# Five z2 normalizes on ScalarE, and three mixing passes of the second token tile written ahead of the last pass of the first

## The chip, the cores and the metric

One core of a Trainium2 chip runs one launch of the kernel. The metric is the device time of that launch in microseconds (us); lower is better. A core has TensorE (PE: matmuls, with PEld for its weight loads), VectorE (DVE), ScalarE (ACT), GpSimd (POOL) and SyncE (SP), which here issues nearly all DMAs. Each engine works through its own queue in order, and an instruction that waits holds up all behind it on its engine.

## The reference

The kernel computes x + A(xn) + B(xn), with xn the layer norm of x (2048 tokens, 512 columns, bf16).

```python
def A(x, wqkv, wo):            # sliding dilated attention: 32 heads of 16, window 8, dilation 2
    q, k, v = heads(x @ wqkv)
    logits = einsum('bhsd,bhswd->bhsw', q, kg) * scale     # kg, vg: k, v at s, s-2, ..., s-14
    attn = softmax(where(mask, logits, -1e9))
    return einsum('bhsw,bhswd->bhsd', attn, vg).reshape(B, S, D) @ wo

def B(x, w_in, w_sp, b_sp, w_out):                         # gated MLP with mixing over tokens
    z = gelu(x @ w_in)                                     # 2048 x 1376
    z1, z2 = z[..., :688], layernorm(z[..., 688:])
    g = einsum('ts,bsf->btf', w_sp, z2) + b_sp[None, :, None]
    return (z1 * g) @ w_out
```

## The kernel before

All tensors stay in SBUF; 2048 tokens are 16 tiles of 128. A tile is named by (j, tb), where tb is one of four blocks of 512 tokens and j one of the four tiles in it. The work of all engines is written out by hand, in one string, `ORDER` (line 41): each word is a step, and the steps are issued in the order of the words. A step puts its instructions at the end of the queues of its engines; there is no scheduler that would change the order. A table `steps` (line 717) maps the first letters of a word to a function.

The steps that matter here, with their engine and line:

- `V`, `X`, `z`, `q` (TensorE): matmuls for v (L431), z1 and z2 (L263), q and k (L321).
- `Vc` and `Xg` (ScalarE): they empty the PSUM tile of a `V` (L437) or, through gelu, of an `X` (L312).
- `zg`, `zs` (ScalarE): gelu of z2 with its sum (L281), square with its sum (L287). `st.0` to `st.4` make mean and 1/std of all 16 tiles from these (L290 to L300).
- `Nj.tb` (VectorE, L304): the normalize of tile (j, tb) of z2, in place: subtract the mean, multiply by 1/std. There are 16.
- `Gn` (TensorE, L470): the mixing matmuls for output tile n, 32 of them in four passes of eight. Pass b, written `Gn.b`, reads the z2 tiles with j = b; in `Gn` alone all four follow each other. `Gin` (ScalarE, L476) adds the bias and empties the PSUM tile; `Un` (VectorE, L484 and L486) multiplies by z1; `Tn` (SyncE, L490) transposes the product by DMA.
- `pg.c`, `ag`, `bg` (VectorE, L361, L370, L373): products of q and k and their sums for group g of the attention. `Lg` (TensorE, L381) sums them over the head's 16 columns into logits, and `Lcg` (ScalarE, L387) empties these.
- `M0.k` (VectorE, L395 to L401), `E0` (ScalarE, L405), `S0.0` to `S0.2` (VectorE, L410 to L414), `S0.3` and `S0.4` (ScalarE, L417 and L420), `R0` (VectorE, L424): the softmax of the first half of the token tiles: maximum, exp, sum, reciprocal as exp of -ln, scaling. `M1`, `E1`, `S1`, `R1` are the second half.
- `An` (VectorE, L445 and L449): attention weights times v, 60 steps.
- `O`, `Or`, `Oh`, `Of` (TensorE, L523, L532, L553): the two output projections, added up in one PSUM tile for each block of 128 tokens. `Or` reads the transposed products that the `T` steps land. `Fe`, `F`, `s` (ScalarE L536, VectorE L541 and L543, SyncE L548) empty it, add x and store.
- `wn` (SyncE, L461): loads the rows of w_sp for `Gn`, transposed. Loads reuse each other's space, so that `w6` waits for the end of `G0`.

Two more things set the order. The gelu and exp functions on ScalarE need different tables, and a table load stands in ScalarE's queue where the kind changes (ahead of `Xg6`, of `E0`, and so on). The PSUM tiles of `V`, `X`, `q`, `z` and `G` come from one pool of three buffers, those of `L` from a pool of two: a matmul that takes a buffer waits until the step on ScalarE that empties it has ended. The matmuls of `L7` take the buffer that `Lc5` gives back.

Of the kernel before, what the change touches and what calls it, by code (L numbers as in the profile page):

```python
# [8 lines left out]
F32 = mybir.dt.float32  # L9
ACT = mybir.ActivationFunctionType  # L10
ALU = mybir.AluOpType
# [3 lines left out]
P = 128  # L15
S = 2048
D = 512
NT = S // P
# [26 lines left out]
b2 zg0.2 zs3.3 L0 L1 Xg4 q3.1 p3.2 zs3.1 p3.0 Lc0 q3.0 Lc1 p3.1 qc3.1 q3.2 p3.3 qc3.0 zs0.1 a3 z0.3 qc3.2 q3.3  # L45
zg0.3 p4.1 zs1.3 p4.0 z0.0 qc3.3 X1 p4.2 zg0.0 zs0.3 X2 p4.3 Xg1 X5 st.0 zs2.1 st.1 a4 Xg2 L2 V6 zs0.2 zs3.2
b3 Xg5 V2 b4 Vc6 zs0.0 p5.3 L3 V5 zs3.0 p5.2 Vc2 V1 st.2 p5.1 Vc5 p5.0 V0 st.3 a5 w4 Lc2 Vc1 V4 st.4 Vc0 w1
N1.1 V3 N2.0 Vc4 N1.0 b5 Lc3 V7 N0.0 Vc3 M0.0 N1.2 M0.1 L5 N0.2 L4 Vc7 N3.3 X6 N0.1 M0.2 N0.3 late X3 N3.1
N1.3 N2.1 G0.0 N2.2 Xg6 N2.3 N3.2 N3.0 G0.1 p7.1 G0.2 M0.3 G0.3 p7.2 G4 p6.0 Gi0 w6 Lc4 p6.3 Xg3 p6.2 E0 p7.3
G3 p6.1 U0 S0.0 p7.0 a6 w9 G1 Gi3 Gi4 S0.1 b6 a7 G2 Gi1 w7 U1 S0.2 b7 S0.3 w5 S0.4 Lc5 R0 L6 L7 G6 Lc6 A0 Gi2  # L50
Lc7 U2 U4 mask T4 U3 M1.0 A1 T2 G7 A2 Gi6 w8 A3 wo1.2 A4 T0 A5 X7 M1.1 Gi7 A6 wo1.3 xr0 G5 A7 Xg7 A8 w10 M1.2
A9 w12 U7 A10 X8 Gi5 A11 X10 T1 A12 G8 Xg10 A13 Xg8 wo1.0 A14 T7 M1.3 A15 G9 Gi8 A16 A17 E1 A18 A19 wo0.2
# [17 lines left out]
def kernel(  # L70
# [13 lines left out]
    V = nc.vector  # L84
    A = nc.scalar
# [8 lines left out]
    sb = ctx.enter_context(tc.tile_pool(name="sb", bufs=1))  # L94
# [44 lines left out]
    z2 = sb.tile([P, NT, FH], BF16, name="z2")  # L139
# [15 lines left out]
    zmean = sb.tile([P, NT], F32, name="zmean")  # L155
    zm2 = sb.tile([P, NT], F32, name="zm2")
    zvar = sb.tile([P, NT], F32, name="zvar")
    zrstd = sb.tile([P, NT], F32, name="zrstd")
    eps_t = sb.tile([P, 1], F32, name="eps_t")
    mhalf = sb.tile([P, 1], F32, name="mhalf")  # L160

# [127 lines left out]
    def z2_var():  # L289
        return [lambda: V.tensor_scalar(zmean[:], zsum[:], 1.0 / FH, None, ALU.mult),  # L290
                lambda: V.tensor_tensor(zm2[:], zmean[:], zmean[:], ALU.mult),
                lambda: V.scalar_tensor_tensor(zvar[:], zsq[:], 1.0 / FH, zm2[:], ALU.mult, ALU.subtract)]
# [9 lines left out]
    def z2_norm(j, tb):  # L302
        i, q = 4 * tb + j, 4 * j + tb
        V.tensor_scalar(z2[:, i, :], z2[:, i, :], zmean[:, q:q + 1], zrstd[:, q:q + 1], ALU.subtract, ALU.mult)  # L304

    def z1_mm(n):
        tiles["x", n] = zmm(4 * (n % 4) + ORD[n // 4], w_z1)
# [99 lines left out]
    def sm_sum(hf, k):  # L407
        a = a_sb[:, :, 256 * hf:256 * hf + 256]
        if k == 0:
            V.tensor_tensor(smt[:], a[:, 0:4, :], a[:, 4:8, :], ALU.add)  # L410
        elif k == 1:
            V.tensor_tensor(smt[:, 0:2, :], smt[:, 0:2, :], smt[:, 2:4, :], ALU.add)
        elif k == 2:
            V.tensor_tensor(smt[:, 0, :], smt[:, 0, :], smt[:, 1, :], ALU.add)  # L414
        elif k == 3:
            need_table("exp")
            A.activation(smt[:, 1, :], smt[:, 0, :], ACT.Ln)  # L417
        else:
            need_table("exp")
            A.activation(srec[:], smt[:, 1, :], ACT.Exp, scale=-1.0)  # L420
# [290 lines left out]
    def halo_zero():  # L711
# [3 lines left out]
    st = z2_var() + [z2_log, z2_exp]  # L715

    steps = {"z": z2_mm, "zg": z2_gelu, "zs": z2_sq, "q": qk_mm, "qc": qk_cast, "p": prod_c, "a": pair_add, "b": pair_add2,
             "L": logits, "Lc": logits_cast, "V": v_mm, "Vc": v_cast, "X": z1_mm, "Xg": z1_gelu,
             "st": lambda k: st[k](), "N": z2_norm,
             "M": sm_max, "E": sm_exp, "S": lambda h, k: sm_sum(h, k), "R": sm_norm, "mask": add_mask,  # L720
             "G": g_mm, "Gi": g_bias, "U": u_mul, "T": u_tr, "A": lambda k: ap[k](),
             "O": out_heads, "Or": out_rest, "Oh": out_half, "Of": out_first, "Fe": out_evac, "F": out_add, "s": out_store, "end": last_adds,
             "halo": halo_zero, "wo": load_wo, "late": load_late, "xr": load_xr, "w": load_wsp}
    for tok in ORDER.split():
        name = tok.rstrip("0123456789.")
# [31 lines left out]
```

## Time and profile before

| what | value |
|---|---|
| time, median of 3 runs | 201.84 us (201.63 to 201.85) |
| span of the profiled execution | 199.9 us, 4102 instructions |
| time around the span (median less span) | 1.94 us |
| TensorE busy | 195.4 us, 98% |
| VectorE busy | 184.6 us, 92% |
| ScalarE busy | 103.9 us, 52% |
| GpSimd busy | 22.0 us, 11% |
| 16 normalizes (L304) | 6.4 us, 0.460 us each |
| 16 bias steps (L476) | 13.2 us, 0.834 us each |
| mixing matmuls, first and last start (L470) | 77.7 and 180.0 us |

The span runs from the first to the last instruction of one profiled execution; starts are counted from its begin. A timeline line gives start, length, engine, source line, operation, output and inputs, and in brackets the idle time of the engine before it and what ended that. Several equal instructions in a row are one line with their count, and its length is that of the whole row; instructions of an engine overlap a little, so that the distance from start to start is less than the length of one.

### The profile page before, as it was taken

How to read it: one execution, taken by the hardware profiler on the slowest of the kernel's cores; microseconds unless marked ns; L12 is line 12 of the kernel's file. 1: busy time of each engine (PE TensorE's matmuls, PEld its weight loads, DVE VectorE, ACT ScalarE, POOL GpSimd, SP SyncE). 2: the span in 40 equal slices, each digit the busy share in tenths (PEclk: the TensorE clock that was granted, in tenths of full speed). 3: DMA queues.
4: the chain of work that ended last, by engine and by line, in shares of the span. 5: the costliest groups of instructions: out<-in, count | busy, mean ns of one | idle time of the engine just before them, and what ended most of it. 6: DMA issues, size and time to landing. Idle time of an engine off the chain costs nothing.

```text
span 199.9 us, 4102 instructions
## 1 busy us (share of the span) xinstructions
PE 195.4 (98%) x1691; PEld 123.9 (62%) x1691; DVE 184.6 (92%) x249; ACT 103.9 (52%) x175; POOL 22.0 (11%) x23
## 2 busy tenths in 40 slices
PE   7899999999999999999999999999999999999994
PEld 2869756665566666666656666666544646664562
DVE  5789899999999999999979999999999999999624
ACT  3586978899899976453431523708402230331400
POOL 3000800699500000000000000000000000000000
DMA  5986548950000096524477999199940297219863
GB/s 160 266 244 163 106 78 240 234 113 3 0 0 3 3 157 115 167 64 100 61 152 161 239 220 192 49 217 180 192 85 0 81 208 169 72 32 127 215 209 105
DMA packets 66562, 25.91 MB, mean 130 GB/s; under 512 B 56496, under 2 KB 66288, under 8 KB 66288
## 3 DMA queue, kind: packets, MB, share of 16 engines
q1 hardware_dynamic: 65824, 25.18, 58.4%
q10 hardware_dynamic: 720, 0.48, 0.8%
q8 instruction: 13, 0.21, 0.4%
q14 instruction: 5, 0.04, 0.1%
HBM read 10.13 MB, written 2.10 MB: 61 GB/s over the span
## 4 chain that ended last, share of the span: by engine, by line
PE 95%; DMA 1%; DVE 1%; SPq 0%; ACT 0%; issue 0%
PE pg L470 37%; PE pz L263 19%; PE pq L321 11%; PE pv L431 7%; PE po L553 7%; PE po L523 6%; PE pa L553 2%; PE pq L327 2%; DMA r_x<-in_A_x_dram 1%; PE pl L381 1%; PE pa L321 1%; PE po L532 1%; PE pb L523 1%; PE pt L238 0%; DVE r_pr L541 0%; DVE stats L213 0%
## 5 line engine op out<-in xcount | busy, mean ns | idle before, releaser
L470 PE MATMUL pg<-z,r_qk 128*128 128x344 bf16 x448 | 66.8, 309 | 0.0
L470 PEld LDWEIGHTS <-r_qk 128*128 128x128 bf16 x448 | 43.8, 98 | 22.0 <-issue 0.4
L445 DVE TENSOR_TENSOR r_pr<-r_x,r_w 128x2048 bf16<-128x2048 bf16 x32 | 38.4, 1220 | 1.3 <-PE pl L381 1.0
L263 PE MATMUL pz<-w_z,xnT 128*128 128x344 bf16 x256 | 39.3, 309 | 0.0
L449 DVE TENSOR_TENSOR r_pr<-r_pr 128x2048 bf16<-128x2048 bf16 x28 | 33.9, 1219 | 0.4
L263 PEld LDWEIGHTS <-xnT 128*128 128x128 bf16 x256 | 25.0, 98 | 13.2 <-issue 0.4
L476 ACT ACTIVATE gs<-pg,b_col 128x688 bf16<-128x688 f32 x16 | 13.2, 834 | 35.4 <-PE pg L470 26.4
L361 DVE TENSOR_TENSOR r_pr<-r_qk 128x2048 bf16<-128x2048 bf16 x24 | 27.9, 1222 | 0.2 <-ACT r_qk L337 0.2
L321 PE MATMUL pq<-xnT,r_w 128*128 128x512 bf16 (+1 forms) x128 | 23.8, 339 | 0.0
L321 PEld LDWEIGHTS <-r_w 128*128 128x128 bf16 x144 | 15.9, 114 | 7.6 <-issue 0.4
L536 ACT CAST r_qk<-po 128x512 bf16<-128x512 f32 x10 | 5.5, 588 | 22.7 <-PE po L553 22.7
L699 POOL CAST b_col<-b 128x16 f32<-128x16 bf16 x1 | 15.7, 15704 | 11.8 <-DMA b<-in_B_b_sp_dram 11.8
L337 ACT CAST r_qk<-pq 128x1024 bf16<-128x1024 f32 x15 | 14.9, 1015 | 2.4 <-PE pq L321 2.3
L312 ACT ACTIVATE r_uz<-pz 128x688 bf16<-128x688 f32 x16 | 11.7, 740 | 6.6 <-PE pz L263 6.5
L523 PE MATMUL po<-r_lg,r_pr 32*128 32x512 bf16 x192 | 14.5, 375 | 0.0
L431 PE MATMUL pv<-xnT,r_w 128*32 128x512 bf16 x256 | 14.2, 379 | 0.0
L553 PEld LDWEIGHTS <-r_uz 128*128 128x128 bf16 x85 | 8.0, 98 | 9.5 <-issue 1.1
L370 DVE TENSOR_TENSOR r_pr<-r_pr 128x4096 bf16<-128x4096 bf16 x6 | 13.7, 2289 | 0.0
L553 PE MATMUL po<-r_w,r_uz 128*128 128x512 bf16 x60 | 13.6, 380 | 0.0
L281 ACT ACTIVATE z<-pz 128x688 bf16<-128x688 f32 x16 | 11.9, 744 | 1.5 <-PE pz L263 1.5
L287 ACT ACTIVATE junk<-z 128x688 bf16<-128x688 bf16 x16 | 12.4, 774 | 0.1
L431 PEld LDWEIGHTS <-r_w 128*32 128x32 bf16 x256 | 9.5, 138 | 4.3
(88 smaller groups left out, 200.3 us busy)
## 6 DMA issues: line engine op xcount, KB each, us to landing
r_lg<-in_A_wo_dram SPq DMA_DIRECT2D x8, 256.0 KB, 4.2
r_x<-in_A_x_dram SPq DMA_DIRECT2D x12, 128.0 KB, 3.0
out_dram<-r_qk SPq DMA_DIRECT2D x12, 128.0 KB, 2.1
r_w<-in_A_wqkv_dram SPq DMA_DIRECT2D x8, 128.0 KB, 3.6
r_qk<-in_A_x_dram SPq DMA_DIRECT2D x8, 128.0 KB, 2.2
w_z<-in_B_w_in_dram SPq DMA_DIRECT2D x4, 172.0 KB, 4.4
w_z<-in_B_w_in_dram SPq DMA_DIRECT2D x1, 688.0 KB, 5.5
r_w<-in_B_w_out_dram SPq DMA_DIRECT2D x1, 640.0 KB, 6.5
```

Source lines behind the costliest of these rows:

```text
L263: PE.matmul(pz[:, hh, 0:FHALF], xnT[:, kc, i * P:(i + 1) * P], wz[:, kc, hh * FHALF:(hh + 1) * FHALF], start=(kc == 0), stop=(kc == C - 1))
L321: PE.matmul(pq[:, cc, p0 * P:(p0 + b1 - b0) * P], wqk[:, sd, kc, c0 + cc:D:C], xv[:, kc, b0:b1, j, :], start=(kc == 0), stop=(kc == C - 1))
L337: cast = A.copy(dst, pq[:, :, p0 * P:(p0 + b1 - b0) * P].rearrange("p c (b t) -> p c b t", b=b1 - b0))
L361: prod = V.tensor_tensor(pr[g % 3][:, c].rearrange("p w b t -> p b w t"), q3.unsqueeze(2).broadcast_to([P, TB, 4, P]), k4, ALU.mult)
L370: V.tensor_tensor(pr[g % 3][:, 0:2], pr[g % 3][:, 0:2], pr[g % 3][:, 2:4], ALU.add)
L431: PE.matmul(pv[32 * tb:32 * tb + 32, dd, :], wv[:, kc, 2 * d2 + dd, :], xnT[:, kc, tb * TBS:(tb + 1) * TBS], start=(kc == 0), stop=(kc == ...
L445: V.tensor_tensor(pw_t[n], vp[:, :, off:off + P], a_sb[:, slot_w(w), ts].unsqueeze(1).broadcast_to([P, DH, P]), ALU.mult)
L449: V.tensor_tensor(pw_t[n] if dst is None else dst, pw_t[n], pw_t[m], ALU.add)
L470: PE.matmul(pg[:, hh, 0:FHALF], wsp[n][:, k, :], z2[:, k, hh * FHALF:(hh + 1) * FHALF], start=(k == 0), stop=(k == NT - 1))
L523: PE.matmul(pc, op[32 * tb:32 * tb + 32, d, o * P:(o + 1) * P], wo_r[32 * tb:32 * tb + 32, d, cs], start=(d == 8), stop=False, tile_positi ...
L553: mm = PE.matmul(pc, uT[:, o % 2, m, tb * P:(tb + 1) * P], wout[:, m, cs], start=False, stop=(m == MCH - 3))
L699: G.tensor_copy(b_col[:], b16[:])
```

## The change

It has three parts, all in the stretch where the first mixing tiles begin.

1. Five of the sixteen normalizes, (2,3), (3,3), (3,1), (3,2) and (3,0), are no longer done by VectorE but by ScalarE, as an Identity activation with a scale and a bias for each partition. The first two stand ahead of `Xg6` in ScalarE's queue, the other three behind it and ahead of `Gi0`. The order of the normalizes left on VectorE changes a little: (2,2) comes before (1,3) and (2,1).
2. A new step `Z` on VectorE makes the bias, -mean/std of all 16 tiles, in one small instruction between the normalizes.
3. Passes 0, 1 and 2 of `G4` are written ahead of pass 3 of `G0`, and pass 3 of `G4` behind it. Before, all four passes of `G4` followed `G0`. Pass 3 reads the tiles (3, 0) to (3, 3), all four of which are now ScalarE's.

```diff
 ORDER (the rows that change)
-N1.1 V3 N2.0 Vc4 N1.0 b5 Lc3 V7 N0.0 Vc3 M0.0 N1.2 M0.1 L5 N0.2 L4 Vc7 N3.3 X6 N0.1 M0.2 N0.3 late X3 N3.1
-N1.3 N2.1 G0.0 N2.2 Xg6 N2.3 N3.2 N3.0 G0.1 p7.1 G0.2 M0.3 G0.3 p7.2 G4 p6.0 Gi0 w6 Lc4 p6.3 Xg3 p6.2 E0 p7.3
+N1.1 V3 N2.0 Vc4 Z N1.0 b5 Lc3 V7 N0.0 Vc3 M0.0 N1.2 M0.1 L5 N0.2 L4 Vc7 NA2.3 NA3.3 X6 N0.1 M0.2 N0.3 late X3 N2.2
+N1.3 N2.1 G0.0 Xg6 NA3.1 NA3.2 NA3.0 G0.1 p7.1 G0.2 M0.3 G4.0 G4.1 G4.2 G0.3 G4.3 p7.2 p6.0 Gi0 w6 Lc4 p6.3 Xg3 p6.2 E0 p7.3
 G3 p6.1 U0 S0.0 p7.0 a6 w9 G1 Gi3 Gi4 S0.1 b6 a7 G2 Gi1 w7 U1 S0.2 b7 S0.3 w5 S0.4 Lc5 R0 L6 L7 G6 Lc6 A0 Gi2
...
+    zshift = sb.tile([P, NT], F32, name="zshift")
...
+    def z2_shift():
+        V.scalar_tensor_tensor(zshift[:], zmean[:], -1.0, zrstd[:], ALU.mult, ALU.mult)
+
+    def z2_norm_act(j, tb):
+        i, q = 4 * tb + j, 4 * j + tb
+        A.activation(z2[:, i, :], z2[:, i, :], ACT.Identity, bias=zshift[:, q:q + 1], scale=zrstd[:, q:q + 1])
...
-             "st": lambda k: st[k](), "N": z2_norm,
+             "st": lambda k: st[k](), "N": z2_norm, "NA": z2_norm_act, "Z": z2_shift,
```

The row that begins with `G3` is unchanged and is shown because the prediction follows it.

## The prediction

> **What bounds the kernel now.** I read the busy times first, then the chain that ended last, then the busy times by stretch, and at last the timelines of ScalarE, VectorE and SyncE around the change.
>
> ```profile
> PE 195.4 (98%) x1691; PEld 123.9 (62%) x1691; DVE 184.6 (92%) x249; ACT 103.9 (52%) x175; POOL 22.0 (11%) x23
> PE 95%; DMA 1%; DVE 1%; SPq 0%; ACT 0%; issue 0%
> ```
>
> TensorE carries the end: 95% of the chain is matmul. The question is whether it ever waits. In order of time, and by stretch (us, PE busy, PEld, DVE, ACT, POOL, clock, DMA share, GB/s):
>
> ```profile
> 77.82 23.33 PE pg L470 x160
> 101.15 0.55 PE pl L381 x8
> 77.60:101.10 23.50, 23.50 (x166) 15.59 (x167) 22.85 (x26) 9.33 (x12) 0.00 (x0) 1.00 0.51 108
> 101.10:142.60 41.50, 41.50 (x293) 27.45 (x296) 40.66 (x49) 18.38 (x22) 0.00 (x0) 1.00 0.91 173
> ```
>
> From 77.6 to 142.6 it is busy throughout, at full clock. The 160 mixing matmuls take 23.33 / 160 = 0.1458 us each without a gap. So nothing around the change holds TensorE today, and an edit there can only leave the time or add a stall. It has to be found which wait now ends last. The starts below are the timeline's (first G0 matmul 77.65). ScalarE:
>
> ```profile
> 82.58 0.83 ACT L476 ACTIVATE gs<-pg,b_col 128x688 bf16<-128x688 f32 x1 [4.51 <-PE pg L470]
> 83.31 0.59 ACT L387 ACTIVATE r_lg<-pl 128x512 bf16<-128x512 f32 x1
> 83.79 0.75 ACT L312 ACTIVATE r_uz<-pz 128x688 bf16<-128x688 f32 x1
> 84.55 1.28 ACT L272 ACT_TABLE_LOAD   x1
> 85.85 1.91 ACT L405 ACTIVATE r_w<-r_lg 128x2048 bf16<-128x2048 bf16 x1
> 98.34 0.42 ACT L417 ACTIVATE smt<-smt 128x256 f32<-128x256 f32 x1 [0.99 <-DVE smt L414]
> 99.11 0.58 ACT L387 ACTIVATE r_lg<-pl 128x512 bf16<-128x512 f32 x1
> ```
>
> These are Gi0, Lc4, Xg3, the table load, E0 (the first exp), S0.3 and Lc5. The bracket says that Gi0 waited for the end of G0, and the four behind it follow without a gap. VectorE:
>
> ```profile
> 88.75 1.22 DVE L410 TENSOR_TENSOR smt<-r_w 128x1024 f32<-128x1024 bf16 x1
> 94.96 2.29 DVE L370 TENSOR_TENSOR r_pr<-r_pr 128x4096 bf16<-128x4096 bf16 x1
> 97.39 0.49 DVE L484 TENSOR_TENSOR r_uz<-gs,r_uz 128x640 bf16<-128x640 bf16 x1
> 97.89 0.42 DVE L414 TENSOR_TENSOR smt<-smt 128x256 f32<-128x256 f32 x1
> 101.53 1.23 DVE L445 TENSOR_TENSOR r_pr<-r_x,r_w 128x2048 bf16<-128x2048 bf16 x1 [0.95 <-PE pl L381]
> 102.89 0.49 DVE L484 TENSOR_TENSOR r_uz<-gs,r_uz 128x640 bf16<-128x640 bf16 x1
> ```
>
> These are S0.0, a7, U1, S0.2, A0 and U2. S0.0 reads what E0 wrote (E0 ends 87.76).
>
> **Part 1: five normalizes leave VectorE.** Eight in a row took 3.04 us with 0.46 for the last, so one costs (3.04 - 0.46) / 7 = 0.37. Five less is 1.85; the new zshift row (like L292, 0.17, taken as 0.2 with its hand-over) leaves 1.65 us. VectorE reaches U0 that much earlier, and there it waits for Gi0. TensorE gains nothing: the last normalize ended at 79.26 and its pass began at 81.15, 1.9 us later. Worth 0; it cannot be a gain while TensorE is gapless.
>
> **Part 2: five normalizes on ScalarE.** No row shows this form. The nearest are L476 (0.83 long; two take 1.56, so 0.73 apart) and the L287 square of the same SBUF tile (0.77). Bounds 0.60 to 0.95 apart; I take 0.73, since L476 is the same function with a pointer operand. NA2.3 and NA3.3 stand before the gelu table load and push Xg6 by 1.5, to an end near 79.5; G4 takes Xg6's PSUM buffer and is due at 81.15. The other three end near 81.8; G0.3 is due at 84.65. Even 0.95 leaves over a microsecond, so the cost is 0; beyond 1.5 apart the excess of two of them would stop TensorE at G4. No table load is added: L476 runs behind either load today. The Trainium skill ("ScalarE: Activation LUTs", What ACT_TABLE_LOAD costs) gives 186 ns + 0.833 ns per element and 93 ns per pointer operand, an estimate of 0.95 us for 688 elements and two pointers, where the L476 row with one pointer took 0.83; both fit into the idle time.
>
> **Part 3: three passes of G4 ahead of the last of G0.** Three passes are 24 matmuls, 24 x 0.1458 = 3.50 us. G0 ends 3.50 later; TensorE's total is the same. But everything queued behind Gi0 on ScalarE moves by 3.50.
>
> First wait: G3 takes G0's PSUM buffer, because Gi0 gives it back before Xg3 gives back X3's. Gi0 ended 82.58 + 0.83 - 82.17 = 1.24 after G0's last matmul began; behind that matmul now stand the eight of G4.3, so G3 is due 9 x 0.1458 = 1.31 after it. Margin 0.07, less a hand-over of about 0.03: cost 0, bounds 0 and 0.1.
>
> Second wait, the one that counts. E0 moves from 85.85 to 89.35 and ends 91.26. VectorE stands at S0.0 (idle about 3.8 us, all that part 1 freed and more) and starts it at 91.28 instead of 88.75: 2.53 late. Behind it stand p7.0, a6, S0.1, b6, a7, U1, S0.2, b7. One gap gives time back: U1 waited for Gi1 until 97.39, while a7 started at 94.96 and such an add takes 2.20 start to start (91.02 to 93.22), so U1 could have started at 97.16: 0.23. S0.2 is then 2.30 late, and so are S0.3, S0.4 and, queued behind these on ScalarE, Lc5, which ends at 99.69 + 2.30 = 101.99. Lc5 empties the PSUM buffer that L7 writes. L7 began at 101.31 (the second four of eight, 101.08 + 0.62 - 0.39), with 1.6 us to spare. Now it is stopped until 102.02: **0.7 us**, and G6 and all later matmuls with it. b7, which L7 reads, ends at 98.22 + 1.22 + 2.30 = 101.74, earlier than that.
>
> The Trainium skill ("ScalarE: Activation LUTs", the same section) puts a table switch at 1.28 us of load plus 1.38 of drain; the row has E0 at 85.85, right behind the load from 84.55, so no drain shows here. By the rule E0 would come 1.38 later and the stall would be an estimated 2.1 us, 203.9 in all.
>
> Third wait: VectorE stays behind. R0 ends at 99.36 + 2.30 + 1.22 = 102.88, A0 starts at 102.90, U2 at 104.04 (1.14 apart): 1.15 late, against 0.7 on TensorE. VectorE is busy 40.66 of 41.50 us up to 142.6, so nothing makes up the 0.43. It matters where TensorE waits for something of VectorE's with less than 0.43 to spare. I went through these: O1 has 0.9, O3 1.1, and one is short:
>
> ```profile
> 178.60 2.57 SPq L490 DMA_TRANSPOSE r_uz<-r_uz  x2
> 183.66 0.60 PE L532 MATMUL po<-r_w,r_uz 24*128 24x512 bf16 x8
> ```
>
> The first of the two transposes (T11) is issued behind a store that waits for VectorE (F1.2), and lands at 183.54 by its landing records; Or2 reads it at 183.67, 0.12 later. With 0.43 the stall is **0.3 us**; bounds 0 (the lag is made up in 75 us, or the landing is set by other traffic) and 0.5 (landing times of these transposes spread from 2.6 to 6.7 us).
>
> SyncE: w6 waits for G0 and moves from 82.51 to 86.0; w9 behind it waited for VectorE until 88.37 and can go at 88.1. Both are due after 101. Cost 0.
>
> **The sum.** 0.7 + 0.3 = 1.0 on a span of 199.9; 1.94 us lie around the span (201.84 - 199.9), so 202.85. Against the median of 201.84 that is +0.5%. About 0.2% (0.4 us) is what this measurement can tell from no change.
>
> **Rivals.**
> - Only the L7 stall: the lag is made up before T11. 201.84 + 0.7 = 202.55. For it: the short margin at Or2 rests on one landing. Chance 0.26.
> - A larger loss: the G3 wait (0.1), a slower T11 (0.5) and a hand-over behind each stall, 1.5 in all, 203.35. Against it: the other waits have 0.9 and more to spare. Chance 0.12.
> - G3 takes X3's buffer after all: Xg3 ends 84.54 + 3.50 = 88.04 and G3, due at 86.99, waits 1.1; L7 is then due at 102.4 and no longer stalls. 202.95. Three buffers taken in turn would do this; in the program as built the buffer first given back is taken. Chance 0.05, within the range.
> - The other side: what the matmul rows hide is a wait for the normalizes (their ends are modelled), and a lighter VectorE pulls in the whole end, as it is 92% busy. Price: the 1.65 us of part 1, 200.2. It decides if the passes begin late because a normalize is late; the 1.9 us between the last normalize and its pass, and starts at an even 0.1458, speak against it. Chance 0.03.
> - No change: the exp's 3.5 us are taken up before Lc5. For this less than 1.6 of the 2.3 may arrive, so another 0.7 has to be made up between S0.0 and S0.2, where one gap of 0.23 shows. 201.84. Chance 0.04.
>
> **How the numbers follow.** Both stalls 0.50; L7 alone 0.26; larger 0.12; the other buffer 0.05: slower by over 0.2% 0.93. No change 0.04, faster 0.03. The range runs from L7 alone at 0.5 (202.35) to the larger loss (203.4), and leaves out about 0.15.
>
> **What would show it.** In the changed profile: G0.0 still at 77.65, and the matmuls gapless up to L6; Gi0 at 86.1, E0 at 89.35; VectorE idle before L410 for almost 4 us, released by ScalarE; TensorE idle 0.7 at the second logits tile near 101.3, released by ScalarE (Lc5), and 0.3 at the L532 matmuls near 184. Wrong if TensorE has no idle time near 101 (then the time is unchanged), or if it stops at G3 near 87, or if mixing starts earlier than 77.65.

## The result and the profile after

The changed kernel takes 202.55 us (median of 7 runs, 202.13 to 202.68) against 201.70 (7 runs, 201.61 to 201.95) of the kernel before in the same session: ratio 1.0039, 95% interval 1.0029 to 1.005. It is slower by 0.8 us; 1.0 was forecast. The profiled execution took 202.65 us with a span of 200.8. New code puts the lines of the changed kernel 1 higher up to the normalizes (L272 is L273) and 8 higher behind them: L470 is L478, L387 is L395, and so on. The ScalarE normalize is L312, which was gelu's line before; that is now L320.

Busy times, and the chain that ended last, of the changed kernel:

```profile
PE 195.2 (97%) x1687; PEld 124.0 (62%) x1691; DVE 182.8 (91%) x245; ACT 108.2 (54%) x180; POOL 22.5 (11%) x23
PE 87%; DVE 5%; DMA 3%; ACT 3%; issue 1%; ACTq 0%
```

Part 1 is visible at once: VectorE is busy 1.8 us less. But the chain, 95% matmul before, is now 87%: VectorE and ScalarE have entered it. The waits of TensorE after 77 us (what it waited for, total, times, longest) have one entry other than `issue`; that query is empty for the kernel before:

```profile
PE pl L389 <- ACT r_lg L395: 0.6, 1, 0.6
```

TensorE's timeline shows the place:

```profile
77.79 9.50 PE L478 MATMUL pg<-z,r_qk 128*128 128x344 bf16 x64
87.12 4.83 PE L478 MATMUL pg<-z,r_lg 128*128 128x344 bf16 x32
...
101.22 0.40 PE L389 MATMUL pl<-r_pr,rsel 128*32 128x512 bf16 x4
102.20 0.40 PE L389 MATMUL pl<-r_pr,rsel 128*32 128x512 bf16 x4 [0.58 <-ACT r_lg L395]
102.53 2.65 PE L478 MATMUL pg<-z,r_qk 128*128 128x344 bf16 x17
```

The eight logits matmuls of L6 and L7 were one row of 0.62 before, with G6 0.55 behind their start (101.08 to 101.63). Now they are torn in two and G6 comes 1.31 behind: 0.76 us lost. (The bracket says 0.58 because it counts from the modelled end of L6.) The bracket names ScalarE's L395, which is Lc5. The last matmul of the kernel starts at 197.81, before at 196.91: 0.90 later, of which 0.14 is start-up (the first mixing matmul at 77.79 for 77.65) and 0.76 the stall. So nothing else was lost in this profile, and the windows agree that it is one place (TensorE busy 41.50 of 41.50 before in the second window, 40.92 now):

```profile
77.60:101.10 23.50, 23.50 (x163) 15.66 (x160) 19.39 (x21) 12.68 (x15) 0.00 (x0) 1.00 0.55 108
101.10:142.60 41.50, 40.92 (x285) 27.22 (x284) 41.12 (x50) 18.73 (x25) 0.00 (x0) 1.00 0.87 174
```

How the stall comes about can be read along the chain, in order of time (start, length, engine, output, line). A piece of the chain begins where the piece ahead of it ends, so that it can start up to 0.1 later than the instruction itself in a timeline:

```profile
86.22 0.12 ACT gs L484
...
88.19 1.28 ACT L273
...
89.48 1.92 ACT r_w L413
...
91.43 1.23 DVE smt L418
92.65 1.14 DVE r_pr L369
93.79 2.20 DVE r_pr L378
...
100.42 0.35 DVE smt L422
...
100.79 0.43 ACT smt L425
...
101.24 0.42 ACT srec L428
101.66 0.50 ACT r_lg L395
...
102.20 0.40 PE pl L389 x4
```

In the timelines Gi0 starts at 86.22 (before 82.58), E0 at 89.48, S0.0 at 91.43, S0.2 at 100.34 and Lc5 at 101.57, and L7 follows it. VectorE's own rows show what became of the time that part 1 freed:

```profile
87.08 0.49 DVE L492 TENSOR_TENSOR r_uz<-gs,r_uz 128x640 bf16<-128x640 bf16 x1 [0.36 <-ACT gs L484]
91.43 1.23 DVE L418 TENSOR_TENSOR smt<-r_w 128x1024 f32<-128x1024 bf16 x1 [3.76 <-ACT r_w L413]
99.85 0.48 DVE L492 TENSOR_TENSOR r_uz<-gs,r_uz 128x640 bf16<-128x640 bf16 x1
```

It stood 0.36 at U0 and 3.76 at S0.0. In front of U1 no idle time is left; that gap has been used up. ScalarE's normalizes, with gelu's Xg6 between them:

```profile
76.04 1.81 ACT L312 ACTIVATE z<-z,zshift,zrstd 128x688 bf16<-128x688 bf16 x2
77.87 1.28 ACT L320 ACT_TABLE_LOAD   x1
79.17 0.74 ACT L320 ACTIVATE r_uz<-pz 128x688 bf16<-128x688 f32 x1
79.81 2.65 ACT L312 ACTIVATE z<-z,zshift,zrstd 128x688 bf16<-128x688 bf16 x3
```

### The profile page after: what moved, and what is told of

Same layout as the page of the kernel before. It is cut to its first block, busy times and chain, and to the rows that moved or that the text cites. A ratio compares the mean times of both kernels' runs of the same rounds, so it can differ in the third digit from the quotient of the medians.

```text
span 200.8 us, 4100 instructions
## 1 busy us (share of the span) xinstructions
PE 195.2 (97%) x1687; PEld 124.0 (62%) x1691; DVE 182.8 (91%) x245; ACT 108.2 (54%) x180; POOL 22.5 (11%) x23
## 4 chain that ended last, share of the span: by engine, by line
PE 87%; DVE 5%; DMA 3%; ACT 3%; issue 1%; ACTq 0%
PE pg L478 30%; PE pz L264 19%; PE pq L329 11%; PE pv L439 7%; PE po L531 6%; PE po L561 6%; DVE r_pr L378 2%; PE pa L561 2%; DMA r_w<-in_A_wqkv_dram 2%; PE pq L335 2%; DMA r_x<-in_A_x_dram 1%; PE pl L389 1%; ACT r_w L413 1%; PE pa L329 1%; PE po L540 1%
## 5 line engine op out<-in xcount | busy, mean ns | idle before, releaser
L478 PE MATMUL pg<-z,r_qk 128*128 128x344 bf16 x448 | 66.8, 309 | 0.0
L478 PEld LDWEIGHTS <-r_qk 128*128 128x128 bf16 x448 | 43.8, 98 | 21.8 <-issue 0.2
L320 ACT ACTIVATE r_uz<-pz 128x688 bf16<-128x688 f32 x16 | 11.7, 740 | 6.6 <-PE pz L264 6.5
L561 PE MATMUL po<-r_w,r_uz 128*128 128x512 bf16 x56 | 12.7, 379 | 0.5 <-issue 0.5
```

Source lines behind the costliest of these rows:

```text
L478: PE.matmul(pg[:, hh, 0:FHALF], wsp[n][:, k, :], z2[:, k, hh * FHALF:(hh + 1) * FHALF], start=(k == 0), stop=(k == NT - 1))
L561: mm = PE.matmul(pc, uT[:, o % 2, m, tb * P:(tb + 1) * P], wout[:, m, cs], start=False, stop=(m == MCH - 3))
```

## The experiments

The theory under test: the loss is one wait, L7's for Lc5, which comes late because three passes ahead of G0's last push Gi0, and all that ScalarE has behind it, by 3.5 us; where the normalizes are done matters only for the order of the passes. The rivals: the normalizes themselves cost time (on ScalarE, or by reading and writing tiles beside other work); each pass costs its share; the loss lies later, behind T11.

All times are medians with the ratio to the kernel before in the same session and its 95% interval. The kernel before took 201.73 (18 runs) beside the order alone, ScalarE's normalizes alone, two passes and four passes; 201.79 (29 runs) beside one pass, the exp early and the two kernels that move Lc5; and 201.55 (9 runs) beside the last two, on T11. Stalls at L7 are worked out as above: G6's start less L6's start, less 0.55. One check covers every profile: from the first mixing matmul to the last matmul of the kernel it takes 119.26 us before, and in each experiment longer by the sum of the stalls named below, to 0.02. So no loss elsewhere behind the start of mixing is left out.

**The order alone.** The kernel before, all sixteen normalizes on VectorE, with the passes in the new order:

```diff
-N1.3 N2.1 G0.0 N2.2 Xg6 N2.3 N3.2 N3.0 G0.1 p7.1 G0.2 M0.3 G0.3 p7.2 G4 p6.0 Gi0
+N1.3 N2.1 G0.0 N2.2 Xg6 N2.3 N3.2 N3.0 G0.1 p7.1 G0.2 M0.3 G4.0 G4.1 G4.2 G0.3 G4.3 p7.2 p6.0 Gi0
```

> Only the order of the passes is changed; all sixteen normalizes stay on VectorE. Theory (the chain from Gi0 over E0, S0.0 and S0.4 to Lc5 holds L7): Gi0 still moves by 3.5 us, E0 ends near 91.3, S0.0 starts there, L7 stalls 0.7 to 0.8 us; 0.7 to 0.8 above before, some 202.45, the same as the whole change. Rival (the work added on ScalarE, or zshift, costs the time): nothing of it is here, 201.7 as before.

202.40 us, 1.0032 (1.0021 to 1.0044). TensorE's timeline (lines as in the kernel before):

```profile
101.55 0.40 PE L381 MATMUL pl<-r_pr,rsel 128*32 128x512 bf16 x4
102.53 0.40 PE L381 MATMUL pl<-r_pr,rsel 128*32 128x512 bf16 x4 [0.58 <-ACT r_lg L387]
102.86 0.90 PE L470 MATMUL pg<-z,r_qk 128*128 128x344 bf16 x5
```

The stall is 0.76 again (102.86 - 101.55 - 0.55) at the same place with the same releaser. The order makes it, and the normalizes on ScalarE are not needed for it. VectorE, with all sixteen normalizes to do, is not idle in front of U0 and less idle in front of S0.0:

```profile
91.76 1.23 DVE L410 TENSOR_TENSOR smt<-r_w 128x1024 f32<-128x1024 bf16 x1 [2.45 <-ACT r_w L405]
```

In the change it stood there 3.76 and 0.36 in front of U0, 1.67 more in all. That is what part 1 freed.

**ScalarE's normalizes alone.** The changed kernel with the passes in the old order:

```diff
-M0.3 G4.0 G4.1 G4.2 G0.3 G4.3 p7.2 p6.0
+M0.3 G0.3 p7.2 G4 p6.0
```

> Only the five normalizes go to ScalarE (with zshift); G4 follows G0 whole, as before. Theory: the last of the five ended at 82.46 in the changed kernel (82.3 without its late start), but G0.3 is due at 81.15, so TensorE stops at G0.3 for 1.2 us; Gi0 and E0 move by only 1.2 and L7, then due 1.2 later as well, does not stall: 1.2 above before, some 202.9, with VectorE in front of L410 idle much less than 3.8 us. Rival (the order of the passes alone costs, the normalizes on ScalarE are free): 201.7.

203.11 us, 1.0068 (1.0056 to 1.0081): worse than both parts together. TensorE's waits after 77 us other than `issue`, its timeline, and ScalarE's last three normalizes:

```profile
PE pg L478 <- ACT z L312: 1.0, 1, 1.0
```

```profile
77.84 3.66 PE L478 MATMUL pg<-z,r_qk 128*128 128x344 bf16 x24
82.55 5.99 PE L478 MATMUL pg<-z,r_qk 128*128 128x344 bf16 x40 [1.05 <-ACT z L312]
...
102.47 0.61 PE L389 MATMUL pl<-r_pr,rsel 128*32 128x512 bf16 x8
```

```profile
79.84 2.65 ACT L312 ACTIVATE z<-z,zshift,zrstd 128x688 bf16<-128x688 bf16 x3
```

After 24 matmuls, that is at pass 3 of G0, TensorE is due at 77.84 + 24 x 0.1458 = 81.34 and starts at 82.55: 1.21 us, waiting for the last of the three normalizes (79.84 + 2.65 = 82.49). The medians are 1.38 apart, and 1.21 lies inside their interval. At L7 nothing is lost. So the normalizes on ScalarE come too late for the old order and need passes of G4 ahead of G0.3 as a cover. The new order needs nothing of the normalizes: it loses 0.76 at L7 with them or without.

**One, two and four passes ahead.** The changed kernel with another number of G4's passes ahead of G0.3:

```diff
-G4.0 G4.1 G4.2 G0.3 G4.3
+G4.0 G0.3 G4.1 G4.2 G4.3      (one)
+G4.0 G4.1 G0.3 G4.2 G4.3      (two)
+G4.0 G4.1 G4.2 G4.3 G0.3      (four)
```

> The whole change, but one pass of G4 ahead of G0.3. Theory: G0.3 is due at 82.3, the last normalize on ScalarE ends there too (82.46 less 0.14), so a stall of 0.1 to 0.2 at G0.3; E0 moves by 1.3, no stall at L7: 201.8. Rival (a share for each pass, 0.27 us): 202.0.

> The whole change, but two passes of G4 ahead of G0.3 instead of three. Theory (a threshold): Gi0 moves by 2.33, E0 ends near 90.1, S0.0 is 1.35 late, 0.23 comes back at U1, Lc5 is 1.1 late, less than the 1.6 that L7 has to spare: no stall, 201.7. Rival (each pass moved costs its share, 0.27 us): 202.2.

> The whole change, but all four passes of G4 ahead of G0.3. Theory: Gi0 moves by 4.67; G3 now begins right behind G0.3 and needs the buffer that Gi0 empties 1.24 after the last matmul began, so it stalls 1.1; Lc5 is 3.5 late, less 1.6 to spare, less the 1.1: L7 stalls 0.7 to 0.8 more. In all 1.8 to 2.0 above before, some 203.6. Rival (a share for each pass, 0.27 us): 202.8.

The starts of S0.0 and Lc5 are counted from the first mixing matmul, since the start-up differs by up to 0.5 us between profiles:

| passes ahead | time, us | ratio (95%) | S0.0 | Lc5 | TensorE stalls |
|---|---|---|---|---|---|
| 0 (the kernel before) | 201.70 | 1 | 11.10 | 21.46 | none |
| 1 | 201.78 | 0.9993 (0.9981 to 1.0006) | 11.36 | 21.51 | G0.3 0.05 |
| 2 | 201.79 | 1.0004 (0.9994 to 1.0014) | 12.48 | 22.61 | none |
| 3 (the change) | 202.55 | 1.0039 (1.0029 to 1.005) | 13.64 | 23.78 | L7 0.76 |
| 4 | 203.63 | 1.0098 (1.0083 to 1.0113) | 14.8 | 24.94 | G3 1.15, L7 0.78 |

The stall of 0.05 at one pass is read from the start of G3, 9.39 behind the first mixing matmul for 9.34 before: one pass covers the normalizes but for that, where without it they cost 1.21. From one pass to two and from two to three Lc5 slips by 1.1 to 1.2, one pass of eight matmuls. Two passes cost nothing and the third costs 0.76: a margin is used up, and no price is paid per pass. L7 is free at a slip of 1.15 and stalls 0.76 at 2.32; if all beyond the margin is paid, the margin is 1.56 (2.32 - 0.76). Four passes agree: a slip of 3.48, less 1.15 for TensorE's own delay at G3, less the stall of 0.78, is 1.55. The prediction read 1.6 from the trace before. With four passes a second wait appears, the one that the prediction gave a margin of 0.07 in the change itself:

```profile
88.19 4.83 PE L478 MATMUL pg<-z,r_lg 128*128 128x344 bf16 x32 [0.98 <-ACT gs L484]
```

This is G3, which waits for Gi0 to give back G0's buffer.

**The exp ahead of Gi0.** The changed kernel with Xg3 right behind Xg6, and Lc4 and E0 ahead of Gi0 in ScalarE's queue, so that the softmax no longer stands behind G0's end:

```diff
-Xg6 NA3.1 NA3.2 NA3.0 ... G0.2 M0.3 G4.0 ... Gi0 w6 Lc4 p6.3 Xg3 p6.2 E0 p7.3
+Xg6 Xg3 NA3.1 NA3.2 NA3.0 ... G0.2 M0.3 Lc4 E0 G4.0 ... Gi0 w6 p6.3 p6.2 p7.3
```

> The whole change, with only ScalarE's queue rewritten: Xg3 right behind Xg6, and Lc4 and E0 right behind the five normalizes, ahead of Gi0. Theory: E0 runs near 85 to 87 while G0 and G4 still go on, VectorE has hardly a wait at S0.0, L7 does not stall: 201.7, all 0.8 us back, although the passes and the five normalizes are as in the change. Gi0 comes some 0.6 late, but G3 then takes the buffer that Xg3 gave back. Rivals (the pass order itself, or the work on ScalarE, costs): still about 202.5.

201.77 us, 1.0001 (0.9988 to 1.0014). The loss is gone with the wait for Gi0. ScalarE's and TensorE's timelines:

```profile
84.91 1.91 ACT L413 ACTIVATE r_w<-r_lg 128x2048 bf16<-128x2048 bf16 x1
86.73 0.82 ACT L484 ACTIVATE gs<-pg,b_col 128x688 bf16<-128x688 f32 x1
```

```profile
101.24 0.61 PE L389 MATMUL pl<-r_pr,rsel 128*32 128x512 bf16 x8
101.79 2.51 PE L478 MATMUL pg<-z,r_qk 128*128 128x344 bf16 x16
```

L6 and L7 are one row again. Nothing is gained below the time before, though VectorE does 1.8 us less: TensorE has no wait left that it could give back.

**Lc5 taken out of the late chain.** First Lc5 alone ahead of S0.3 in ScalarE's queue; then b7 on VectorE, which L7 reads, ahead of U1 and S0.2 as well:

```diff
-a7 G2 Gi1 w7 U1 S0.2 b7 S0.3 w5 S0.4 Lc5 R0 L6 L7
+a7 G2 Gi1 w7 U1 S0.2 b7 Lc5 S0.3 w5 S0.4 R0 L6 L7      (Lc5 early)
+a7 b7 G2 Gi1 w7 U1 S0.2 Lc5 S0.3 w5 S0.4 R0 L6 L7      (Lc5 and b7 early)
```

> The whole change, with Lc5 moved ahead of S0.3 in ScalarE's queue. Theory: L7's buffer is free by 98, and the next that ends last is b7 on VectorE (100.68 + 1.22 in the changed kernel), so the stall at L7 shrinks from 0.76 to about 0.5 and is now released by VectorE; 202.2 to 202.25. If Lc5 was not what held L7: no change, 202.5. If Lc5 alone held it: 201.7.

202.20 us, 1.002 (1.0008 to 1.0032). The wait has another releaser, b7 on VectorE, and is 0.51 (102.16 - 101.10 - 0.55):

```profile
101.83 0.40 PE L389 MATMUL pl<-r_pr,rsel 128*32 128x512 bf16 x4 [0.34 <-DVE r_pr L381]
102.16 2.07 PE L478 MATMUL pg<-z,r_qk 128*128 128x344 bf16 x13
```

> As with Lc5 moved, and b7 also moved, ahead of U1 and S0.2 on VectorE. Theory: L7 no longer stalls, but S0.2, S0.3, S0.4, R0 and A0 come 1.14 later still, VectorE is then 2.2 us behind and stays so, and TensorE stops where it has less to spare: X12 (1.7 spare, Xg9 behind S1.4) 0.5, O1 (0.9 spare, A29) 0.7, and Or2 up to 0.7 if T11's landing follows its issue: 202.9 to 203.6. Rival (VectorE's lag is made up over the following 70 us): 201.7 to 201.9.

203.18 us, 1.007 (1.0051 to 1.0089): L7 no longer waits (L6 and L7 are one row of 0.61), and the kernel is slower than the change. The waits of TensorE after 77 us other than `issue`:

```profile
PE po L531 <- DVE r_pr L457: 0.6, 1, 0.6
PE pz L264 <- ACT r_uz L320: 0.6, 1, 0.6
```

They are at X12 (141.17, 0.74 lost, 0.5 forecast) and O1 (148.30, 0.8 lost, 0.7 forecast), 40 us later. X12 waits for a gelu that stands on ScalarE behind the second softmax, whose sums come from VectorE; O1 waits for VectorE itself. In the kernel before the distance to O1 was 0.9 by the prediction. So VectorE's lateness is not made up in between: with the stall at L7 gone, TensorE runs ahead and meets it at the next places. In the changed kernel TensorE too comes later, and neither wait shows there. This edit does not take away L7's wait alone, though: with b7 ahead of it, S0.2 starts 23.81 behind the first mixing matmul, where it started 22.55 behind it in the change. How much of the 1.54 lost is due to this extra 1.26 is not shown. At Or2 nothing was lost here, though T11 left later than in the changed kernel (its times are in the table below).

**T11.** In the changed kernel no wait shows at Or2, where 0.3 was forecast. One kernel swaps the two transposes behind the store s1.2, so that T11 leaves later; the other issues T11 ahead of that store:

```diff
-U14 Gi13 F1.3 F1.2 A53 s1.2 T11 A54 T14 A55 O2
+U14 Gi13 F1.3 F1.2 A53 s1.2 T14 A54 T11 A55 O2      (T11 late)
+U14 Gi13 F1.3 F1.2 A53 T11 s1.2 A54 T14 A55 O2      (T11 early)
```

> The changed kernel with the two transposes of r_uz behind the store s1.2 in the other order (T14, then T11), so that T11 leaves SyncE 1.27 us later than in the changed kernel, about 181.25 instead of 179.97. Theory (a landing follows its issue after 3.5 to 3.8 us here, and the store row Or2 has 0.76 us to spare behind T11's landing): T11 lands at 184.75 to 185.05, Or2 is due at 184.56 and starts 0.1 later than the landing, so TensorE stands 0.3 to 0.6 in front of Or2, and the time is 202.85 to 203.15. Rival (other traffic on the queues holds both transposes, and both land when it lets go, near 183.8): no stall at Or2, 202.55.

> The changed kernel with T11 issued ahead of the store s1.2, behind T12: about 175.1 instead of 179.97, so that T11 has landed long before Or2 reads it. Theory (T11 costs the changed kernel nothing, as no stall is seen at Or2): 202.55, the same as the changed kernel. Rival (T11's landing holds TensorE for part of a third wait that the trace does not show as a gap): up to 0.3 us less, 202.25. For the duration: T14 is then alone behind s1.2 at 179.97; if the pair of transposes slows itself, it lands some 2.6 to 3.0 us after issue, near 182.8; if other traffic slows it, after 3.5 to 4.9 us, near 183.5 to 184.8.

T11 late: 202.72 us (202.09 to 202.78), 1.005 (1.0036 to 1.0064), below the 202.85 to 203.15 of the theory; but the kernel before took 201.55 beside it, and 1.17 above that is the 0.76 at L7 and what is lost at Or2. T11 early: 202.62 us (202.59 to 202.70), 1.0053 (1.0039 to 1.0067). T11's issue and landing in five profiles, and Or2's start:

| kernel | T11 issued | landed | took | Or2 starts | spare |
|---|---|---|---|---|---|
| before | 178.60 | 183.54 | 4.94 | 183.66 | 0.12 |
| the change | 179.97 | 183.80 | 3.83 | 184.56 | 0.76 |
| Lc5 and b7 early | 181.28 | 184.92 | 3.63 | 185.50 | 0.58 |
| T11 late | 181.08 | 184.73 | 3.64 | 184.39 | -0.34 |
| T11 early | 175.22 | 177.85 | 2.63 | 184.60 | 6.75 |

Late, it lands as the first theory said, and Or2's eight matmuls take 0.98 instead of 0.60, with this entry of idle time in front of their weight loads (L540):

```profile
184.39 0.98 PE L540 MATMUL po<-r_w,r_uz 24*128 24x512 bf16 x8
```

```profile
  DMA r_uz<-r_uz: 0.5, 1
```

So TensorE does wait for T11 when it lands late, and this costs 0.38 us in the trace. The medians of the two kernels differ by only 0.10, within the spread of the first, so the times alone would not show it. Early, T11 is out of the way, the trace loses 0.76 as in the change, and the time is not lower: the profiled run of the change loses nothing at Or2. In this kernel T14 was alone behind the store and still took 4.19 (180.03 to 184.21), between the 3.49 (the change) and the 4.46 (the kernel before) that it took behind T11, so that the pair does not explain the long landings.

The other profiles show how little one landing says. In ten kernels T11 is the first transpose behind the store:

| T11 issued, us behind the first mixing matmul | took, us |
|---|---|
| 100.9 to 101.0 | 4.94 (before), 4.88 (one pass), 4.25 (exp early), 4.13 (two passes) |
| 102.1 to 102.2 | 3.83 (the change), 3.65 (order alone), 3.66 (Lc5 early), 4.67 (ScalarE's normalizes alone) |
| 103.3 | 4.11 (four passes), 3.63 (Lc5 and b7 early) |

Issued at the same point it differs by 0.8 to 1.0 from profile to profile, and the 4.94 of the kernel before is the longest of all. None of these kernels stalls at Or2. What makes a transpose take 2.63 at 175 and 3.6 to 4.9 at 179 to 181 stays open.

## Why the prediction was right, and where it was not

- **Part 1, worth 0:** shown. VectorE freed 1.67 us (1.65 forecast), and all of it went into idle time at U0 and S0.0; where TensorE's wait is taken away (the exp early; two passes) the time is the old one and no lower.
- **Part 2, cost 0:** right, with a size off. The normalize took 0.949 on ScalarE, and a row of three 2.65, so (2.65 - 0.949) / 2 = 0.85 apart; 0.73 was taken, from L476, within bounds of 0.60 to 0.95. The Trainium skill ("ScalarE: Activation LUTs", What ACT_TABLE_LOAD costs), by its cost of an activation with two pointer operands, had an estimate of 0.95 for the length; the measurement agrees with it. The cover that was named, G0.3 moved back by 3.5 us, is what hides it: without it 1.21 us are lost. The prediction did not ask how much cover is needed; one pass, 1.17 us, is nearly enough, and the third pass is the one that costs.
- **Part 3, first wait, cost 0:** right. G3 follows at 87.12 without a gap; a fourth pass opens this wait at 1.15.
- **Second wait, 0.7:** measured 0.76. Each step was right to 0.1 when counted from the first mixing matmul: Gi0 3.50 late, S0.0 2.54 (2.53 forecast), S0.2 2.31 and Lc5 2.32 (2.30 for both). So U1's gap of 0.23 was the only time given back, as forecast.
- **The table load:** no drain behind it, again: the load runs from 88.19 for 1.28 and E0 starts at 89.48. The page's 1.38 us of drain, which would have made the stall 2.1, is not seen.
- **Third wait, 0.3:** this term of the sum failed; in the profile it measured 0. Its first half held: T11 left 1.23 later by the start of mixing (1.37 less 0.14) and TensorE was 0.76 late, a lag of 0.47 for the 0.43 forecast. The second half, that the landing moves with the issue, did not: T11 landed only 0.26 later (0.12 by the start of mixing), and Or2 had 0.76 to spare where it had 0.12. One landing was taken as a fixed duration of 4.94, and that was the longest of ten; why it was so long stays open. The rival with the L7 stall alone, at a chance of 0.26, was right that nothing is lost at Or2. The lag was not made up, as it supposed; its remark that the short margin rests on one landing was the point.
- **The number:** that 202.85 lies above the measured 202.55 by just the 0.30 of the failed term, and that this rival named 202.55, is in part luck. The forecast started from 201.84, and the kernel before took 201.70 beside the change; the loss by the medians is 0.85, where the profile shows 0.76.

## What to carry to other kernels

When work is put in front of the end of an accumulation, cost everything that is queued behind the step that empties it, down to the last buffer that another matmul waits for; here the shift was free up to the margin there and paid in full beyond it. Where one edit is only there to cover another, ask how much cover is needed: one pass ahead hid the late normalizes but for 0.05, and the third paid 0.76 for nothing. A wait that is taken away pays if nothing else is late: it did with the exp early, and with Lc5 early until b7 ended last; moving b7 as well made another chain later, and cost more than the wait did.

## What the runs showed of the hardware

In five kernels the DMA transpose T11 of one and the same tile landed 2.63, 3.63, 3.64, 3.83 or 4.94 us after its issue; issued at the same point of the kernel it differed by 0.8 to 1.0 between profiles. Issued 1.37 us later in the change than before, it landed only 0.26 later. One landing time in one trace is no duration to add to.

An activation with two pointer operands on 688 elements took 0.949 us on ScalarE, and three in a row stood 0.85 apart.
